# The second half of the queries in chunks of 256 instead of 512, in an attention + FFN kernel on one core

## The chip, the cores and the metric

The kernel runs on one core of one Trainium2 chip. The metric is the device time of one execution, in microseconds. Nearly all numbers below are medians of several executions, or come from one profiled execution (the span from its first to its last instruction is some 2 us shorter than its time).

The engines are called by their short names: PE is the matmul engine (TensorE), PEld its weight loads, DVE is VectorE, ACT is ScalarE, and SP issues most of the DMAs.

## The reference

S = 2048 tokens, D = 512, 32 heads of 16, an FFN of width F = 1792. All inputs are bfloat16.

```python
def _A_ref(x, wqkv, wo):                       # attention
    qkv = (x @ wqkv).reshape(B, S, 3, H, Dh).transpose(2, 0, 3, 1, 4)
    q, k, v = qkv[0], qkv[1], qkv[2]
    scores = einsum("bhqd,bhkd->bhqk", q, k) * (Dh ** -0.5)
    o = einsum("bhqk,bhkd->bhqd", softmax(scores), v)
    return o.transpose(0, 2, 1, 3).reshape(B, S, D) @ wo
def _B_ref(x, w_gate, w_up, w_down):           # gated FFN
    g = einsum("bsd,df->bsf", x, w_gate)
    u = einsum("bsd,df->bsf", x, w_up)
    return einsum("bsf,fd->bsd", sigmoid(g) * u, w_down)
x = A_x
h = x + _A_ref(_layernorm(x), A_wqkv, A_wo)
h2 = h + _B_ref(_layernorm(h), B_w_gate, B_w_up, B_w_down)       # the output
```

## The kernel before

The exponentials are the bulk of it: 32 heads x 2048 keys x 2048 queries. They are dealt out in **units** of 128 keys x 512 queries of one head, 2048 units in all. ACT does most of them with its Exp function, two or three units per instruction. DVE does 482 of them with integer arithmetic that leaves two operands to be summed up, so a DVE unit gives two value matmuls where an ACT unit gives one. PE makes the scores and the value sums and, in its gaps, everything else.

A head is only 16 wide, so one matmul would use a small part of the 128 x 128 array. Four heads are worked on side by side: head `j` of a group has rows 32j to 32j+31 of the array for its scores, and columns 32j to 32j+31 for its values. I call such a quarter a **strip**; `tile_position` names it.

```python
    QC = 512                # queries in a chunk
    NQC = S // QC           # four chunks
...
    def scores(n):          # the score matmuls of the n-th exponential instruction
        tiles.append(pick(want_dve(n)))
        ...
        for ui, (qc, g, kt, j) in enumerate(tiles[n]):     # chunk, group, key tile, strip
            mm = nc.tensor.matmul(pss[:, ui, :],
                                  lhsT=KT[g // 2][32 * j:32 * j + 32, kt * P:(kt + 1) * P],
                                  rhs=q[32 * j:32 * j + 32, :],
                                  start=True, stop=True, tile_position=(32 * j, 0))
...
    def in_rows(uns, limit):            # order of a batch of value matmuls: strip after strip
        out, rows, left = [], 0, list(uns)
        while left and len(out) < limit:
            used = set()
            for un in list(left):
                if un.u[3] not in used and len(out) < limit:
                    used.add(un.u[3]); left.remove(un); out.append(un)
            rows += 1
        return out, rows

    def av(limit, loose=60.0):          # a batch of value matmuls
        ...
        for un in uns:
            nc.tensor.matmul(acc[32 * j:32 * j + VW, :], lhsT=Vaug[:, kt, h, :], rhs=un.ap,
                             start=(c == 0), stop=(todo[qc, g, j] == 0), tile_position=(0, 32 * j))
...
    NPT, NPE = 36, 14                   # buffers for exponentials: 36 units, 14 more early on
```

The program's order is made ahead of time by a small scheduler in Python, which keeps an estimated clock for each engine and puts PE work between two score batches as long as it fits. Its main loop is this:

```python
        while T["P"] < lim - 100:
            ...
            r = ready_bg(0)             # first item of the background queue
            if early_on or (r is not None and tokens >= bg[0][2][1] and room("dense") >= bg[0][2][0]):
                used = try_bg(tokens, depth=3 if early_on else 1)
                ...
            uns, rows = in_rows(av_ready(60.0), 12)
            last = 0 < len(uns) == av_last()
            fit = int(room("av") // MM) * 4
            if (len(uns) >= 4 or last) and fit >= 4 and av(min(12, fit)):
                continue
            if quiet() and room("dense") >= MM and stir():      # a filler matmul
                continue
            T["P"] += 100
```

The background queue holds projections, and, once a chunk of queries has its attention, that chunk's output projection, layer norm and FFN. In the later part of the program the background has a single PSUM bank of 128 x 512 values. An FFN step fills it with a gate tile, ACT takes it out (tanh), then PE fills it with the up tile and DVE takes it out (product):

```python
    def ffn_up(qc, f):
        ...
        ps = pm_tile()                       # waits until the bank has been emptied
        gate_mm(ps, wgu[:, 0], ...)          # four 512-wide matmuls
        ja = pm_out(act(478, lambda: th.update({f: tanh_out(ps)}), st["mark"]))
        yield pe(2, pm_new)
        ps2 = pm_tile()                      # the same bank
        gate_mm(ps2, wgu[:, 1], ...)
        pm_out(dve(603, lambda: glu_out(hT, f, th[f], ps2), st["mark"], ja))
```

The FFN of the *last* chunk has no attention left to hide behind. After the last exponential comes a **tail**: last values, output projection, layer norm, gate/up, down, all for 512 queries.

## Time and profile before

| | before |
|---|---|
| time, median of 20 runs | 846.7 us (842.4 to 850.1) |
| span of the profiled run | 844.4 us |
| 1024 of 2048 exponential units started | 410.8 us |
| last unit started | 787.6 us |
| from there to the end (the tail) | 56.8 us |

The first fence is the page of the kernel before: the span, each engine's busy time and share of the span, and two of its groups of instructions (line, engine, operation, out<-in, shapes, count, then busy time, mean ns of one, and idle time just before them).

```profile
span 844.4 us, 14580 instructions
PE 757.3 (90%) x5697; PEld 232.8 (28%) x5792; DVE 779.5 (92%) x1446; ACT 765.8 (91%) x783; POOL 2.9 (0%) x7
...
L1189 ACT ACTIVATE pt<-PS 128x1024 f16<-128x1024 f32 (+2 forms) x663 | 699.8, 1190 | 28.4 <-PE PS L938 22.1
L1048 DVE TENSOR_SCALAR J<-PS 128x512 int16<-128x512 f32 x482 | 317.6, 683 | 14.8 <-PE PS L938 8.7
```

The three engines seem about equally busy. The view by windows separates the stages. Its columns are the window, its length, then busy time and instructions of each engine, the granted PE clock, the DMA share and GB/s. The windows are first half, second half and tail.

```profile
core 0: us, PE busy (x) PEld busy (x) DVE busy (x) ACT busy (x) POOL busy (x), PEclk, DMA share, GB/s
0.00:411.00 411.00, 356.81 (x2711) 107.55 (x2756) 385.07 (x730) 376.79 (x382) 2.90 (x7) 0.98 0.09 29
411.00:788.00 377.00, 353.33 (x2759) 104.17 (x2802) 371.90 (x674) 370.42 (x371) 0.00 (x0) 1.00 0.09 28
788.00:845.00 57.00, 47.12 (x233) 21.03 (x234) 22.53 (x44) 18.54 (x32) 0.00 (x0) 0.97 0.21 68
```

In the second half ACT and DVE are busy 98% and 99% of the time: the exponentials bound it. The tail is PE's: 47 of 57 us. PE's 353 of 377 us in the second half is not a measure of its need, because matmuls overlap, as the timeline of the kernel before shows (start, length, engine, line, operation, count):

```profile
330.81 0.39 PE L938 MATMUL PS<-QT_92,KT_86 32*128 32x512 bf16 x3
331.13 1.04 PE L710 MATMUL PS<-xnT_80,wgu 128*128 128x512 bf16 x4
332.10 0.39 PE L938 MATMUL PS<-QT_92,KT_86 32*128 32x512 bf16 x3
...
802.32 20.88 PE L710 MATMUL PS<-xnT_80,X 128*128 128x512 bf16 x94 [0.68 <-DVE xnT_80 L1328]
826.49 12.25 PE L1341 MATMUL PS<-wd,hT 128*128 128x512 bf16 x54
```

Three score matmuls on three strips together take 0.39 us, no longer than one takes: they start 3 to 4 ns apart. Four dense ones take 1.04 us, because dense matmuls start 216 ns apart. The Trainium skill ("Perfetto Trace Analysis", section Identifying the Most-Contended Engine) says that the busy share of the matmul row is not a good measure of how close PE is to its limit, because pipelined instructions look smaller in the trace. The last two lines are the gate/up and down matmuls of the tail, 20.9 and 12.3 us.

### The profile page before, as it was taken

To read this page: it belongs to the slowest core of one execution; us is meant where nothing else is said; L and a number is where in the kernel's file an instruction comes from. 1 tells how busy PE (TensorE), PEld (TensorE's weight loads), DVE (VectorE), ACT (ScalarE), POOL (GpSimd) and SP (SyncE) were. 2 spreads that over 40 slices of the span, in tenths; PEclk is the share of its full clock that TensorE was granted. 3 is DMA by queue.
4 is the path that set the end of the run, shared out by engine and by line. 5 is a ranking of instruction groups with operands and counts; after the bars stand their busy time and mean duration, and the time that the engine had idled before them with its cause. 6 is when DMAs were issued, how large, how long until landed. Compare 5 with 4: busy or idle time off the path is not lost.

```text
span 844.4 us, 14580 instructions
## 1 busy us (share of the span) xinstructions
PE 757.3 (90%) x5697; PEld 232.8 (28%) x5792; DVE 779.5 (92%) x1446; ACT 765.8 (91%) x783; POOL 2.9 (0%) x7
## 2 busy tenths in 40 slices
PE   4878988898899988999999999999898999998897
PEld 1322222222222222222222322222323222222343
DVE  7869899999999999999999999999999999999831
ACT  5839999899999999999999999999899999999631
POOL 1000000000000000000000000000000000000000
PEclk9978999999999999999999999999999999999999
DMA  6020000200000000020100011120100101000500
GB/s 211 1 88 1 1 1 1 63 2 1 2 1 1 14 1 26 26 63 27 51 13 26 2 39 37 51 63 15 38 14 1 51 26 50 1 8 13 175 7 28
DMA packets 38218, 26.16 MB, mean 31 GB/s; under 512 B 2560, under 2 KB 38144, under 8 KB 38144
## 3 DMA queue, kind: packets, MB, share of 16 engines
q1 hardware_dynamic: 36512, 23.99, 9.2%
q10 hardware_dynamic: 1632, 1.18, 0.4%
q8 instruction: 47, 0.77, 0.4%
q14 instruction: 27, 0.22, 0.1%
HBM read 23.07 MB, written 2.10 MB: 30 GB/s over the span
## 4 chain that ended last, share of the span: by engine, by line
DVE 34%; ACT 32%; PE 23%; issue 10%; DMA 0%; ACTq 0%; DVEq 0%
ACT pt L1189 28%; DVE J L1048 13%; DVE X L1082 6%; PE PS L710 6%; PE PS L938 6%; PE PS L1026 5%; DVE X L1072 3%; DVE X L1077 3%; ACT pe L1189 2%; PE PS L727 2%; DVE hT L722 2%; PE PS L1341 1%; DVE xs L982 1%; DVE Vaug L261 1%; PE PS L257 1%
## 5 line engine op out<-in xcount | busy, mean ns | idle before, releaser
L1189 ACT ACTIVATE pt<-PS 128x1024 f16<-128x1024 f32 (+2 forms) x663 | 699.8, 1190 | 28.4 <-PE PS L938 22.1
L1048 DVE TENSOR_SCALAR J<-PS 128x512 int16<-128x512 f32 x482 | 317.6, 683 | 14.8 <-PE PS L938 8.7
L1026 PE MATMUL PS<-pt,Vaug 128*17 128x512 f16 x1502 | 200.0, 383 | 3.1 <-DVE xs L982 2.3
L1082 DVE TENSOR_TENSOR X<-J,X 128x1024 f16<-128x1024 f16 (+1 forms) x246 | 159.2, 671 | 0.0
L1026 PE MATMUL PS<-X,Vaug 128*17 128x512 f16 x964 | 136.9, 383 | 6.1 <-DVE X L1082 2.6
L1026 PEld LDWEIGHTS <-Vaug 128*17 128x17 bf16 x2530 | 61.5, 89 | 127.7 <-issue 100.0
L710 PE MATMUL PS<-xnT_80,wgu 128*128 128x512 bf16 x304 | 88.3, 382 | 2.8 <-DVE hT L722 1.0
L1077 DVE TENSOR_SCALAR X<-J 128x2048 int16<-128x2048 int16 (+3 forms) x126 | 83.3, 661 | 0.1
L1072 DVE TENSOR_SCALAR X<-J 128x2048 int16<-128x2048 int16 (+3 forms) x126 | 83.0, 659 | 0.0
L722 DVE SCALAR_TENSOR_TENSOR hT<-th,PS 128x512 bf16<-128x512 f32 x56 | 38.1, 680 | 15.1 <-PE PS L710 15.1
L738 ACT ACTIVATE th<-PS 128x512 f32<-128x512 f32 x56 | 36.0, 643 | 14.7 <-PE PS L710 14.7
L727 PE MATMUL PS<-wd,hT 128*128 128x512 bf16 x157 | 45.2, 383 | 1.5 <-issue 1.3
L534 PE MATMUL PS<-wo_sb 128*128 128x512 bf16 x129 | 43.3, 393 | 1.7 <-issue 1.4
L938 PEld LDWEIGHTS <-KT_84 32*128 32x128 bf16 x512 | 21.0, 91 | 83.3 <-issue 77.7
L938 PE MATMUL PS<-QT_90,KT_85 32*128 32x512 bf16 x256 | 36.4, 387 | 6.7 <-ACT pt L1189 5.0
L938 PE MATMUL PS<-QT_92,KT_86 32*128 32x512 bf16 x256 | 36.1, 382 | 5.6 <-ACT pt L1189 4.5
L938 PE MATMUL PS<-QT_93,KT_86 32*128 32x512 bf16 x256 | 35.4, 383 | 5.6 <-ACT pt L1189 5.0
L938 PEld LDWEIGHTS <-KT_86 32*128 32x128 bf16 x512 | 19.5, 90 | 75.6 <-issue 75.1
L938 PEld LDWEIGHTS <-KT_85 32*128 32x128 bf16 x512 | 20.0, 91 | 73.5 <-issue 72.3
L938 PE MATMUL PS<-QT_95,KT_87 32*128 32x512 bf16 x256 | 35.7, 382 | 4.9 <-ACT pt L1189 3.8
L938 PE MATMUL PS<-QT_91,KT_85 32*128 32x512 bf16 x256 | 35.1, 382 | 5.1 <-ACT pt L1189 4.2
L938 PEld LDWEIGHTS <-KT_87 32*128 32x128 bf16 x512 | 19.8, 91 | 72.0 <-issue 71.2
(207 smaller groups left out, 575.5 us busy)
## 6 DMA issues: line engine op xcount, KB each, us to landing
wgu<-in_B_w_gate_dram SPq DMA_DIRECT2D x21, 256.0 KB, 2.8
wgu<-in_B_w_up_dram SPq DMA_DIRECT2D x21, 256.0 KB, 3.2
out_dram<-ob SPq DMA_DIRECT2D x16, 128.0 KB, 1.7
wd<-in_B_w_down_dram SPq DMA_DIRECT2D x1, 1792.0 KB, 7.3
xr<-in_A_x_dram SPq DMA_DIRECT2D x12, 128.0 KB, 3.1
X<-in_B_w_gate_dram SPq DMA_DIRECT2D x3, 512.0 KB, 3.8
X<-in_B_w_up_dram SPq DMA_DIRECT2D x3, 512.0 KB, 4.8
wv_sb<-in_A_wqkv_dram SPq DMA_DIRECT2D x1, 512.0 KB, 5.9
```

Source lines behind the costliest of these rows:

```text
L534: nc.tensor.matmul(PS[:, 1 + (st["ring"] + 1) % st["R"], :], lhsT=wo_sb[:, 0, 0:P], rhs=wo_sb[:, 0, :], start=True, stop=True)
L710: nc.tensor.matmul(ps, lhsT=w[:, d, :], rhs=hnT[:, d, :], start=(d == 0), stop=(d == DC - 1))
L722: nc.vector.scalar_tensor_tensor(out=hT[:, f, :], in0=th[:], scalar=1.0, in1=ps, op0=ALU.add, op1=ALU.mult)
L727: nc.tensor.matmul(ps, lhsT=hT[:, f, i * P:(i + 1) * P], rhs=wd[:, f, :], start=(f == 0), stop=(f == FC - 1))
L738: nc.scalar.activation(out=th[:], in_=ps, func=ACT.Tanh, scale=0.5)
L938: mm = nc.tensor.matmul(pss[:, ui, :], lhsT=KT[g // 2][32 * j:32 * j + 32, kt * P:(kt + 1) * P], rhs=q[32 * j:32 * j + 32, :], start=True, ...
L1026: nc.tensor.matmul(acc[32 * j:32 * j + VW, :], lhsT=Vaug[:, kt, h, :], rhs=un.ap, start=(c == 0), stop=(todo[qc, g, j] == 0), tile_positio ...
L1048: nc.vector.tensor_scalar(out=J[:, k, :], in0=src, scalar1=ZOFF, scalar2=0.0, op0=ALU.add, op1=ALU.max)
L1072: V.tensor_scalar(out=X[:, 0, 0:k, :], in0=J[:, 0:k, :], scalar1=POWER, scalar2=LITTLE, op0=ALU.bitwise_and, op1=ALU.bitwise_or)
L1077: V.tensor_scalar(out=X[:, 1, 0:k, :], in0=J[:, 0:k, :], scalar1=FRACTION, scalar2=HALF, op0=ALU.bitwise_and, op1=ALU.bitwise_or)
L1082: V.tensor_tensor(out=x, in0=J[:, a:b, :].bitcast(FP16), in1=x, op=ALU.mult)
L1189: ex = nc.scalar.activation(out=pt, in_=pss[:, 0:wa, :], func=ACT.Exp, scale=AS)
```

## The change

The intent is to halve the tail. If the last chunk has 256 queries, only their output projection, layer norm and FFN remain after the last exponential, and the other 256 can hide in the main loop. The last 1024 queries become four chunks of 256 (`SPAN` 2). To keep exponential instructions as long as they were, a unit then holds *two* key tiles x 256 queries. So what was one 512-wide matmul becomes two 256-wide ones, and they are issued as neighbours on the same strip. Along with it come changes in the scheduler's rules. Cut to its core:

```diff
+    SPAN = [1, 1] + [2] * (2 * (NQC - 2))      # chunks of 512, 512, 256, 256, 256, 256
+    CW = [QC // s for s in SPAN]               # their widths
...
 # scores: a unit is SPAN[qc] key tiles
-            mm = nc.tensor.matmul(pss[:, ui, :], lhsT=KT[...][..., kt * P:(kt + 1) * P],
-                                  rhs=q[32 * j:32 * j + 32, :], ..., tile_position=(32 * j, 0))
+            for i in range(SPAN[qc]):
+                k = kt * SPAN[qc] + i
+                nc.tensor.matmul(pss[:, ui, i * CW[qc]:(i + 1) * CW[qc]],
+                                 lhsT=KT[g // 2][32 * j:32 * j + 32, k * P:(k + 1) * P],
+                                 rhs=q[32 * j:32 * j + 32, cols(qc)],
+                                 start=True, stop=True, tile_position=(32 * j, 0))
...
 # values: the same, two neighbours on one strip
+            for i in range(SPAN[qc]):
+                nc.tensor.matmul(acc[32 * j:32 * j + VW, 0:w], lhsT=Vaug[:, kt * SPAN[qc] + i, h, :],
+                                 rhs=un.ap[:, i * w:(i + 1) * w], ..., tile_position=(0, 32 * j))
...
 # FFN: two feature tiles (each 128 x 256) share one bank, one tanh and one product
+            nc.vector.scalar_tensor_tensor(out=hT[:, f:f + k, cols(qc)],
+                in0=th[f][:].rearrange("p (k n) -> p k n", k=k), in1=ps2.rearrange(...), ...)
...
 # value batches only in full rows of four heads, but for the last of a group
-    def in_rows(uns, limit):
+    def in_rows(uns, limit, full=False):
+            if full and len(row) < live:
+                break
...
 # background: look one item deeper, let the item that holds the open bank go first,
 # put the job that empties the bank at the head of DVE's queue, projection + norm at the front
     def try_bg(tokens, loose=60.0, depth=1):
-        for i in range(depth):
+        owner = next((i for i, item in enumerate(bg) if item is st["open"]), None)
+        for i in range(depth) if owner is None else (owner,):
...
     def pm_out(job):
+        if job in dq:
+            dq.remove(job)
+            dq.insert(0, job)
...
-                queue(wo_ln(qc), ("wo", qc), 24)
+                queue(wo_ln(qc), ("wo", qc), 6 * k, 0)
...
 # main loop
-            r = ready_bg(0)
-            if early_on or (r is not None and tokens >= bg[0][2][1] and room("dense") >= bg[0][2][0]):
-                used = try_bg(tokens, depth=3 if early_on else 1)
+            if early_on or room("dense") >= (bg[0][2][0] if ready_bg(0) is not None else 2 * MM):
+                used = try_bg(tokens, depth=3 if early_on else 2)
...
-            if (len(uns) >= 4 or last) and fit >= 4 and av(min(12, fit)):
+            if fit >= 4 and av(min(12, fit), full=not last):
...
 # a second buffer for the rows h takes room from the exponentials' buffers
-    NPT, NPE = 36, 14
+    NPT, NPE = 30, 14
...
 # tail: 2 instead of 4 tiles of 128 queries
-    qc = NQC - 1
+    qc = NCH - 1
+    n = CW[qc] // P
```

Not shown in the cut are two more marks in the scheduler's list `STAGES`, by which it paces the background. From here on, "order rules" means the four scheduler changes: full rows, deeper look-ahead with the open bank's owner first, the promoted job, and the earlier projection and norm.

## The prediction

> **What bounds it now.** In the stage table (40 us stretches) from 200 to 760 us, ACT and DVE are each busy 39 to 40 of 40 us: the exponentials. PE shows 35 to 38.8 of 40, but its records overlap, so I added up what it really needs from start-to-start times in the trace: dense 128x512 matmuls start 216 ns apart; score or value matmuls on different 32-wide strips of the array start 3 to 4 ns apart (median 4 ns); two in succession on the same strip 215 ns apart (43 value pairs); a change between score, value and dense work costs about 95 ns. For the last 1024 queries (about 410 to 788 us) this gives 336 us of 378: PE has only some 11% to spare. After that comes a tail of 56 us (timeline: gate/up 20.9, down 12.3).
>
> **What the change moves.**
> - Tail: the last FFN serves 256 queries instead of 512. Gate/up 20.9 -> about 12 us, down 12.3 -> 6: about -18 us with the norm. The other half goes into the main loop.
> - ACT and DVE in the main loop: instruction counts of both programs show exponentials about equal (482 -> 470 units on DVE, ACT a little more), 7 more tanh/multiply pairs, 16 more group ends at half width, two more layer norms. Estimate +8 us on each.
> - PE: every 512-wide score or value matmul of the last two blocks becomes two of 256, and the program issues these two **one after the other on the same strip**, then goes to the next strip. PE starts in order: at 662.33 us a value matmul whose strip had been free for 0.19 us and that waited for no semaphore started only behind one held by its own busy strip. The Trainium skill ("TensorE: Matmul & The Clock Gate", Part 3) says the same: matmuls start and end in strict program order. So the second of a pair waits about 108 ns (half of 215) and holds back the next strip. Three score units: 108x4 = 432 instead of 222 ns. Four value units: 430 to 540 instead of 225 ns.
>
> Sum for the last 1024 queries, same rules applied to the new order: scores 76 -> 148 us, values 92 -> 157 (190 without the full-row rule), dense 105 -> 114, switches 63 -> 65: 336 -> 484 us.
>
> **Critical path.** 484 us is over ACT's and DVE's about 385, so PE becomes the bound in the second half, with some waits (94 to 97% useful): 500 to 515. First half hardly changed, 405 to 410. Total 407 + 504 + 38, plus 3 between span and time: 952 us.
>
> **What would show it.** Second half: ACT and DVE fall to about 75% busy, PE 95 to 100%; ACT's and DVE's idle time ends on score matmuls. Same-strip 256-wide neighbours start about 108 ns apart, and the next strip's 3 ns after the second. Last score matmul at about 915 us instead of 787; from there to the end about 38 instead of 56 us. First 400 us within 10 us of before.
>
> **What would make it wrong.** If the array let another strip start past a waiting matmul, PE would need about 345 us, and the result would be about 840: -18 tail, +8 main loop. If waits between PE and ACT add up in the static order (value batches of up to 40), 990.

## The result, and the profile after

| | before | after |
|---|---|---|
| time, median | 846.7 us (20 runs) | 837.0 us (10 runs, 835.1 to 840.8) |
| 1024 units started | 410.8 us | 408.7 us |
| last unit started | 787.6 us | 793.7 us |
| end of the last instruction | 844.4 us | 831.8 us |
| second half of the main loop | 376.8 us | 385.0 us |
| tail | 56.8 us | 38.1 us |

The ratio is 0.9895, with a 95% interval of 0.9875 to 0.9916. Here and below, a ratio is the mean time of one kernel's runs over that of the other's in the same rounds, so it isn't quite the ratio of the quoted medians. The result is a gain of 1%, where I had predicted a loss of 12%.

The page of the kernel after:

```profile
span 831.8 us, 19743 instructions
PE 727.4 (87%) x8183; PEld 288.4 (35%) x8275; DVE 779.2 (94%) x1525; ACT 766.0 (92%) x786; POOL 2.9 (0%) x7
...
L1233 ACT ACTIVATE pt<-PS 128x1024 f16<-128x1024 f32 (+2 forms) x661 | 706.3, 1253 | 29.6 <-PE PS L971 19.0
L1092 DVE TENSOR_SCALAR J<-PS 128x512 int16<-128x512 f32 x470 | 311.4, 681 | 11.9 <-PE PS L971 6.0
```

The windows of the kernel after, again first half, second half and tail:

```profile
0.00:409.00 409.00, 347.96 (x2743) 108.93 (x2792) 387.06 (x736) 375.64 (x383) 2.91 (x7) 0.99 0.10 31
409.00:794.00 385.00, 350.01 (x5220) 161.26 (x5268) 375.26 (x750) 377.18 (x377) 0.00 (x0) 1.00 0.16 46
794.00:832.00 38.00, 29.39 (x232) 18.21 (x225) 16.92 (x41) 13.19 (x28) 0.00 (x0) 0.92 0.31 100
```

PE has nearly twice the matmuls in the second half (5220 for 2759), and its row is no fuller than before (350 us). ACT and DVE are still 98% and 97% busy. So the main loop is bound by the exponentials as it was, and the tail is 19 us shorter. What went wrong with the prediction's sum is to be seen in the timeline of the kernel after:

```profile
599.38 0.84 PE L1069 MATMUL PS<-pt,Vaug 128*17 128x256 f16 x24
600.15 0.40 PE L971 MATMUL PS<-QT_88,KT_84 32*128 32x256 bf16 x6
600.48 0.41 PE L1069 MATMUL PS<-pt,Vaug 128*17 128x256 f16 x8
...
807.25 11.08 PE L724 MATMUL PS<-xnT_82,X 128*128 128x256 bf16 x96 [0.61 <-DVE xnT_82 L1358]
820.25 5.99 PE L1370 MATMUL PS<-wd,hT 128*128 128x512 bf16 x27
```

Six score matmuls, issued as pairs on three strips, are done in 0.40 us. One takes 0.27, so the last of the six started at most 0.13 us after the first. The starts in the trace are these, in ns after the first one, at 600.15 us:

```
record       1    2    3    4    5    6
start        0    6   13  120  125  132
```

The program's order is strip a, a, b, b, c, c. If matmuls started in that order, the second would have to wait some 109 ns for its own strip (half of the 216 of a 512-wide one), the third would start right behind it, and the last of the six would start after 334 ns. What the records show is three that start at once and three more a matmul later: each strip takes its own matmuls in order, and none waits for another strip.

The names in the records show the same without any timing. The built program issues one batch of eight value matmuls as four that read `X` (strips 0, 0, 64, 64) and then four that read `pt` (96, 96, 32, 32). In the trace of the kernel after, two of the `pt` ones start some 100 ns before the last two `X` ones:

```profile
761.26 0.28 PE L1069 MATMUL PS<-X,Vaug 128*17 128x256 f16 x2
761.27 0.28 PE L1069 MATMUL PS<-pt,Vaug 128*17 128x256 f16 x2
761.37 0.28 PE L1069 MATMUL PS<-X,Vaug 128*17 128x256 f16 x2
761.39 0.28 PE L1069 MATMUL PS<-pt,Vaug 128*17 128x256 f16 x2
```

Names out of the order of issue stand in 100 of the 353 value batches of this trace, and in 39 of the 330 of the kernel before: that trace held the answer before the prediction was made.

Over the whole trace, for every batch of one length, I compared the time from the first to the last start with both rules (the rules are computed with 109 ns between starts on a strip and 3 ns between strips):

| 256-wide batch, kernel after | measured median, ns | all in program order | order within a strip only |
|---|---|---|---|
| 6 score matmuls | 134 | 334 | 109 |
| 8 value matmuls | 134 | 446 | 109 |
| 16 value matmuls | 353 | 894 | 328 |
| 24 value matmuls | 571 | 1343 | 546 |
| 40 value matmuls | 1008 | 2240 | 982 |

With the right-hand rule PE's need for the last 1024 queries is 333 us before and 326 us after. With the middle rule it is 336 and 484, the two numbers of the prediction. (The Trainium skill, "TensorE: Matmul & The Clock Gate", Part 1, gives N / 2.4 GHz plus about 2.5 ns between starts, which is 215.8 ns for 512 and 109 for 256. The traces agree with both. For 512, (20.88 - 0.38) us over 95 steps in the tail before is 216 ns; these are 96 matmuls, of which two records are missing. For 256, dense ones in the second half after start mostly 109 ns apart, and in the batches of 24 the second matmul of a strip starts 114 ns after its first and each further one 109. In the tail after the mean is 114 ns, (11.08 - 0.27) us over 95 steps, because some of its steps take 131 to 152.)

### The profile page after: what moved, and what is told of

Same layout as the page of the kernel before. It is cut to its first block, busy times and chain, and to the rows that moved or that the text cites. A ratio compares the mean times of both kernels' runs of the same rounds, so it can differ in the third digit from the quotient of the medians.

```text
span 831.8 us, 19743 instructions
## 1 busy us (share of the span) xinstructions
PE 727.4 (87%) x8183; PEld 288.4 (35%) x8275; DVE 779.2 (94%) x1525; ACT 766.0 (92%) x786; POOL 2.9 (0%) x7
## 4 chain that ended last, share of the span: by engine, by line
ACT 39%; DVE 26%; PE 24%; issue 9%; DMA 1%; SPq 0%; ACTq 0%; DVEq 0%
ACT pt L1233 35%; DVE J L1092 10%; PE PS L971 7%; PE PS L743 5%; PE PS L724 4%; DVE X L1126 4%; PE PS L1069 3%; ACT pe L1233 2%; DVE hT L795 2%; DVE X L1116 2%; DVE X L1121 2%; ACT th L754 1%; PE PS L262 1%; DVE xs L1019 1%; DVE Vaug L266 1%
## 5 line engine op out<-in xcount | busy, mean ns | idle before, releaser
L1069 PE MATMUL PS<-pt,Vaug 128*17 128x256 f16 (+1 forms) x2300 | 175.6, 308 | 1.6 <-DVE xs L1019 1.4
L1069 PE MATMUL PS<-X,Vaug 128*17 128x256 f16 (+1 forms) x1410 | 138.6, 311 | 4.8 <-DVE X L1116 2.8
L1069 PEld LDWEIGHTS <-Vaug 128*17 128x17 bf16 x3777 | 83.8, 89 | 105.8 <-issue 96.9
L1121 DVE TENSOR_SCALAR X<-J 128x2048 int16<-128x2048 int16 (+2 forms) x127 | 81.7, 643 | 0.1
L1116 DVE TENSOR_SCALAR X<-J 128x2048 int16<-128x2048 int16 (+2 forms) x127 | 81.7, 643 | 0.0
L724 PE MATMUL PS<-xnT_80,wgu 128*128 128x256 bf16 (+1 forms) x325 | 60.5, 311 | 1.4 <-DVE hT L795 0.2
L724 PEld LDWEIGHTS <-wgu 128*128 128x128 bf16 x560 | 45.6, 98 | 44.3 <-issue 30.4
L743 PE MATMUL PS<-wd,hT 128*128 128x512 bf16 x182 | 52.9, 383 | 0.7 <-issue 0.5
L971 PEld LDWEIGHTS <-KT_84 32*128 32x128 bf16 x768 | 23.7, 91 | 78.7 <-issue 72.8
L971 PEld LDWEIGHTS <-KT_85 32*128 32x128 bf16 x768 | 25.1, 91 | 71.0 <-issue 68.8
L754 ACT ACTIVATE th<-PS 128x512 f32<-128x512 f32 (+1 forms) x63 | 41.1, 653 | 7.1 <-DVE hT L737 7.1
L971 PEld LDWEIGHTS <-KT_86 32*128 32x128 bf16 x768 | 24.4, 91 | 65.5 <-issue 64.2
L971 PE MATMUL PS<-QT_90,KT_85 32*128 32x256 bf16 (+1 forms) x384 | 36.0, 310 | 12.6 <-ACT pt L1233 11.3
L971 PEld LDWEIGHTS <-KT_87 32*128 32x128 bf16 x768 | 23.1, 91 | 63.6 <-issue 62.6
L971 PE MATMUL PS<-QT_91,KT_85 32*128 32x256 bf16 (+1 forms) x384 | 35.6, 310 | 10.7 <-ACT pt L1233 9.5
L971 PE MATMUL PS<-QT_95,KT_87 32*128 32x256 bf16 (+1 forms) x384 | 36.6, 308 | 7.1 <-ACT pt L1233 6.1
L971 PE MATMUL PS<-QT_92,KT_86 32*128 32x256 bf16 (+1 forms) x384 | 35.5, 308 | 7.3 <-ACT pt L1233 6.7
L971 PE MATMUL PS<-QT_94,KT_87 32*128 32x256 bf16 (+1 forms) x384 | 36.8, 308 | 5.6 <-ACT pt L1233 4.6
L971 PE MATMUL PS<-QT_93,KT_86 32*128 32x256 bf16 (+1 forms) x384 | 36.0, 308 | 6.3 <-ACT pt L1233 5.1
```

Of the source, the lines that this page charges most:

```text
L724: nc.tensor.matmul(ps[:, 0:CW[qc]], lhsT=w[:, d, :], rhs=HN[qc][:, d, cols(qc)], start=(d == 0), stop=(d == DC - 1))
L743: nc.tensor.matmul(ps, lhsT=hT[:, f, q:q + P], rhs=wd[:, f, :], start=(f == 0), stop=(f == FC - 1))
L754: nc.scalar.activation(out=th[:, 0:ps.shape[-1]], in_=ps, func=ACT.Tanh, scale=0.5)
L971: nc.tensor.matmul(pss[:, ui, i * CW[qc]:(i + 1) * CW[qc]], lhsT=KT[g // 2][32 * j:32 * j + 32, k * P:(k + 1) * P], rhs=q[32 * j:32 * j + ...
L1069: nc.tensor.matmul(acc[32 * j:32 * j + VW, 0:w], lhsT=Vaug[:, kt * SPAN[qc] + i, h, :], rhs=un.ap[:, i * w:(i + 1) * w], start=(c + i == 0 ...
L1116: V.tensor_scalar(out=X[:, 0, 0:k, :], in0=J[:, 0:k, :], scalar1=POWER, scalar2=LITTLE, op0=ALU.bitwise_and, op1=ALU.bitwise_or)
```

## The experiments

Twelve kernels were run. Each diff is against the kernel after, but for one that is said to be against the kernel before. "1664 units" and "last unit" are times in the profiled run at which that many exponential units had been started.

### 1. e1: the two halves of a pair not as neighbours

```diff
-            for i in range(SPAN[qc]):
-                nc.tensor.matmul(..., tile_position=(32 * j, 0))
+        for ui, i in sorted(((ui, i) for ...), key=lambda e: (e[1], e[0])):   # all first halves, then all second
+                nc.tensor.matmul(..., tile_position=(32 * j, 0))
 # the same in each row of the value matmuls
```

> The changed kernel, but the two 256-wide matmuls of a unit are no longer neighbours: score tiles and rows of value units go first half of every strip, then second half of every strip. Theory A (each 32-wide strip of the array takes its matmuls in its own order; a busy strip does not hold up the others): no change, ratio to before 0.985 to 0.993, and score tiles of six matmuls still span about 135 ns from first to last start. Theory B (strict program order over all strips, the rule of the prediction): the second of a pair holds up the next strip in the changed kernel and not here, so this should be clearly faster than the changed kernel, by 5% or more.

Measured: 836.6 us, ratio 0.987 (0.985 to 0.990), like the kernel after. Its value batches of 8, 16 and 24 span 125, 343 and 561 ns, each some 10 ns less than in the kernel after. In-order starts would have made this kernel far faster than the kernel after; putting the pairs apart changes nothing that can be seen in the time. So the order of the strips within such a short stretch is free.

### 2. e2: value batches sorted by strip

```diff
-        for un in uns:
+        for un in sorted(uns, key=lambda un: un.u[3]):
```

A batch of 24 now has six matmuls on one strip, then six on the next, and so on.

> The changed kernel, but every batch of value matmuls is issued strip by strip (all of strip 0, then all of strip 1 and so on), so up to six neighbours (256 wide) or three (512 wide) lie on one strip. Theory A without a limit on how far ahead the array looks: no change, 0.985 to 0.993 of before. Theory A with a short look-ahead (a few matmuls): batches of 24 take longer than their 546 to 570 ns, the kernel is slower than the changed one by 2 to 10%. Theory B: value batches run almost one strip after another, about 150 us more PE time in all, about 960 us or more.

Measured: 854.1 us, ratio 1.008 (1.006 to 1.011): some 17 us slower than the kernel after. The last unit started at 816.8 us and the tail was unchanged (36.7 us). Batches of 16 (runs of four on one strip) span 372 ns, as good as the 353 of mixed order. Batches of 24 (runs of six) span 1237 ns instead of 571. The starts of such a batch begin with 0, 115, 224, 230, 334, 344, 443: the second strip begins two matmuls late. The window of the second half:

```profile
412.00:817.00 405.00, 374.55 (x5211) 181.75 (x5252) 379.57 (x750) 381.08 (x378) 0.00 (x0) 1.00 0.15 43
```

ACT's share falls to 94% over these 405 us. Some 36 batches of 24, each 0.67 us longer, make 24 us at most, and the second half of the main loop took 19 us more than after (404.4 to 385.0). So order across strips is free only over a short look-ahead.

### 3. e8: runs of five on one strip

```diff
+        # five neighbours on one strip, then the next strip; what is left over after them
+            place[k] = (seen[p] // 5, p, k)
+        for i, k, kw in sorted(emit, key=lambda e: place[e[1]]):
```

> The changed kernel, value batches issued in runs of five neighbours on one strip, then five on the next strip, then what is left. Rule to be tested, from the second experiment, where runs of four cost nothing (batch of 16: 372 ns) and runs of six made a batch of 24 take 1238 instead of 571 ns: on each strip one matmul runs and three wait, a fourth waiting one blocks all that follow. Then a batch of 24 takes about 8 x 109 = 872 ns plus some start gaps, 870 to 910. If four may wait, 571 to 600; if two, about 1200. One time near 845 us.

Measured in one look: 844.1 us (a single run, so its state isn't known). Batches of 24 span 909 ns, batches of 16 again 372. With e2 this fixes the depth for these value matmuls. If one matmul of a strip runs and three more can wait without holding back other strips, then a run of five delays the next strip by one matmul, a run of six by two. For the last start of a batch of 24 that makes, with 109 ns each, 3 x 1 + 5 = 8 steps = 872 ns for fives, and 3 x 2 + 5 = 11 steps = 1199 ns for sixes. Measured: 909 and 1237. Runs of four cost nothing (372 ns). The kernel after puts only two on a strip before it goes on to the next, so it lies well within this. Whether it is the matmuls themselves that are counted, or the weight load that goes with each, these runs do not show.

### 4. e3 and e6: the order rules alone, with chunks of 512

```diff
-    SPAN = [1, 1] + [2] * (2 * (NQC - 2))
+    SPAN = [1] * NQC
 # and the tail of the kernel before, for 512 queries
```

> The changed kernel's order rules (full value rows of four heads, layer norm first in the background, background look-ahead of two, the second normalised-input buffer) with four chunks of 512 and the old end for 512 queries. If the gain comes from the shorter end (56.8 to 38.1 us in the two traces), paid back in part by the main loop of the last two blocks (+8 us), then this keeps only the 2 us that the first half won, perhaps a little more in the second: 842 to 846 us, ratio 0.994 to 0.999, with an end of about 56 us. Rival: the order rules bring the gain, then this is at 0.99 or below with the end still at 56 us.

Measured: 848.3 us, ratio 1.001, and a **wrong result** (relative error 0.24). The load of the last residual rows went into a buffer that the last query projections still needed: it was issued at 588 us and the projections lasted to 626 us. The time missed the expectation, too (842 to 846 us). The mended kernel puts them elsewhere:

```diff
-    xl = xnT[3]
+    xl = xnT[2]
```

> The third experiment again with its fault mended (the residual rows of the last chunk are loaded into a buffer that is no longer read, the result must be right). Times as there: ratio 0.999 to 1.003, end about 57 us, main loop 788 to 791 us. So the order rules alone gain nothing. Rival: they gain 3 us or more.

Measured: correct, 846.6 us, ratio 1.001 (0.999 to 1.003). The last unit starts at 786.9 us, and the tail is 57.2 us, as before. The order rules with the 30 buffers make no difference to the kernel before.

### 5. e10: the kernel before with 30 buffers

```diff
 # against the kernel before
-    NPT, NPE = 36, 14
+    NPT, NPE = 30, 14
```

> The kernel before, with 30 instead of 36 buffers for exponentials (the changed kernel gave six up for a second buffer of residuals). If the fewer buffers are what made the fifth experiment slow, this is slower than before by 0.3% or more. If not: ratio 0.998 to 1.002.

Measured: 855.5 us, ratio 1.0084 (1.0056 to 1.0112); last unit at 797.7 us. So six fewer buffers cost the old kernel 0.8%, and e6 is "no change" only because the order rules pay that back.

### 6. e5: the chunks of 256 alone, with the old order rules

```diff
-        if job in dq: dq.remove(job); dq.insert(0, job)
-        owner = next((i for i, item in enumerate(bg) if item is st["open"]), None)
-                queue(wo_ln(qc), ("wo", qc), 6 * k, 0)
+                queue(wo_ln(qc), ("wo", qc), 6 * k)
-                used = try_bg(tokens, depth=3 if early_on else 2)
+                used = try_bg(tokens, depth=3 if early_on else 1)
-            if fit >= 4 and av(min(12, fit), full=not last):
+            if (len(uns) >= 4 or last) and fit >= 4 and av(min(12, fit)):
```

> The changed kernel's four chunks of 256 and its shorter end, but with the order rules of before: any four value units are issued at once instead of full rows of four heads, background work is taken only from the head of its list, the layer norm waits its turn. Theory C (the gain is the shorter end alone; the rules only move work): end 38 us, main loop as long as in the changed kernel or up to 3 us longer, 836 to 841 us, ratio 0.988 to 0.993. Rival D (the chunks need the full rows, because value matmuls in broken rows cost PE time when PE has little to spare): main loop 8 us or more longer, ratio 0.997 or above.

Measured: 851.1 us, ratio 1.0053 (1.003 to 1.0076). The last unit starts at 804.6 us, 11 us later than in the kernel after, and the tail is 44 us. A part is one stall, shown by a window and by the waits from 446 to 456 us of this kernel (engine, line, what it waited for, total us, times, longest):

```profile
448.00:454.00 6.00, 1.67 (x22) 0.71 (x25) 4.79 (x19) 0.38 (x1) 0.00 (x0) 0.79 0.01 1
...
ACT pt L1229 <- PE PS L1065: 6.4, 1, 6.4
...
PE PS L1065 <- DVE X L1122: 3.4, 1, 3.4
```

ACT waits 6.4 us for an exponential buffer to be freed by value matmuls (line 1065), and these wait for a DVE product, which stands behind the small steps of a layer norm in DVE's queue. Nothing like it is in the second half of the kernel after, whose longest wait of ACT for value matmuls is 2.3 us. Of the 11 us, 4.2 arise before the 1024th unit (412.9 us; 408.7 in the kernel after), where the chunks are 512 wide in both, and 6.7 in the second half, where the stall is. The 6 us of the tail I did not take apart. Theory C (836 to 841 us) missed; the size was that of rival D, but e9 below speaks against the full rows as its reason.

With e6 and e10 this gives a table of two by two, all four with 30 buffers (ratio to the kernel before with its 36):

| | old order rules | new order rules |
|---|---|---|
| chunks of 512 | 1.0084 (e10) | 1.0009 (e6) |
| last 1024 queries in chunks of 256 | 1.0053 (e5) | 0.9895 (the kernel after) |

One way to add it up: +0.84% for the buffers, -0.75% for the order rules, -1.14% for the chunks. The chunks by themselves gain 0.31% with the old rules, so most of their gain depends on the new ones. Two reservations: the 0.31% are not clear of noise (the intervals of e5 and e10 overlap, and they ran in different rounds), and e10 is the kernel before, so it differs from e6 in the pacing marks and the second buffer for `h` as well as in the order rules.

### 7. e4: only the last 512 queries in chunks of 256

```diff
-    SPAN = [1, 1] + [2] * (2 * (NQC - 2))
+    SPAN = [1] * (NQC - 1) + [2, 2]
```

> Only the last 512 queries are split in two chunks of 256; the block before goes as one chunk of 512. The end stays at 38 us. Splitting one block less saves 8 pairs of group ends (0.58 us of DVE each pair by the trace: 2 x 1.15 instead of 1.72 us, estimate 4.6 us), one set of small layer-norm steps and weight loads: if these are what the main loop pays, this is 2 to 4 us faster than the changed kernel, ratio to before 0.984 to 0.988. Rival: small chunks help the main loop by themselves (work of the FFN spread evenly), then it is slower than the changed kernel, 0.991 or more.

Measured: correct, 845.3 us, ratio 0.999 (0.997 to 1.001). The expectation missed; the rival was right. At 1664 units this kernel was ahead (646.6 us; after 650.5), and at the last unit it was behind (799.8; after 793.7). The windows from there to the last unit, first of this kernel, then of the kernel after:

```profile
646.00:800.00 154.00, 141.80 (x2013) 63.41 (x2037) 145.11 (x283) 144.45 (x150) 0.00 (x0) 0.97 0.17 50
```

```profile
650.00:794.00 144.00, 133.16 (x2057) 65.76 (x2071) 140.39 (x270) 141.19 (x144) 0.00 (x0) 1.00 0.20 57
```

For the same number of units it has 10 us more, in which DVE is busy 5 us more and ACT 3 us more, and both have idle time (94%). In these last 512 queries it has to hide the FFN of 768 queries (a whole chunk of 512 and then one of 256), where the kernel after hides that of 512. That this is the cause is my reading; no run changes the FFN's load alone. The clock also dipped in this profile (0.97).

### 8. e7: one feature tile of 256 in a bank

```diff
     def ffn_up(qc, f):
-        k, w = SPAN[qc], CW[qc]
+        k, w, m = 1, CW[qc], 2 // SPAN[qc]
 # one tile per bank, one tanh and one product for each; estimates halved
```

> The changed kernel, but in the chunks of 256 the FFN takes one feature tile (256 wide) per PSUM bank instead of two. In the main loop 21 tanh and 21 products of 512 become 42 and 42 of 256: by the trace 0.37 instead of 0.60 us and 0.42 instead of 0.68 us each, so about 3 us more of ACT and 3.4 us more of DVE. If ACT and DVE are the bound: 2 to 4 us slower than the changed kernel, ratio 0.992 to 0.995. If the single bank that the background has left makes twice as many turns a wait for PE: 6 us or more slower.

Measured: 865.0 us, ratio 1.021 (1.019 to 1.024), the slowest of all: without this part the change loses 2%. The rival was right, and its size was well above its lower bound of 6 us. At the last unit (804.7 us) a part of the background FFN was left over and ran alone. The window and the timeline there:

```profile
805.00:868.00 63.00, 46.03 (x303) 27.25 (x293) 19.79 (x48) 16.30 (x36) 0.00 (x0) 0.78 0.27 85
...
814.51 1.01 PE L724 MATMUL PS<-xnT,wgu 128*128 128x256 bf16 x4 [0.58 <-DVE hT L737]
...
815.57 0.38 ACT L754 ACTIVATE th<-PS 128x256 f32<-128x256 f32 x1 [2.69 <-PE PS L724]
816.00 1.01 PE L724 MATMUL PS<-xnT,wgu 128*128 128x256 bf16 x4 [0.47 <-ACT th L754]
...
817.12 0.42 DVE L737 SCALAR_TENSOR_TENSOR hT<-th,PS 128x256 bf16<-128x256 f32 x1 [2.66 <-PE PS L724]
```

The one bank is filled (1.01 us), emptied by ACT (0.38), filled (1.01), emptied by DVE (0.42), with nothing beside it: 3.1 us for 128 features of 256 queries. PE's granted clock is low there (0.78 over the window, 0.50 from 812 to 819 us; that the gaps are the reason is my reading), and four 256-wide matmuls take 1.01 us, where four of them at full clock (at 601.63 us of the kernel after) take 0.61. The bank is turned over as often for 256 queries as for 512 if it holds one tile; with two tiles in it the number of turns per query stays what it was.

### 9. e9: batches of any rows

```diff
+            uns, rows = in_rows(av_ready(60.0), 12)
-            if fit >= 4 and av(min(12, fit), full=not last):
+            if (len(uns) >= 4 or last) and fit >= 4 and av(min(12, fit)):
```

> The changed kernel with one of its order rules undone: value matmuls are issued again as soon as four units are ready, in whatever rows they make. The fifth experiment (all order rules undone) lost 1.6% on the changed kernel, in part by one stall of 7 us near 450 us where background order matters. If the full rows are what PE needs in the chunked blocks: value time rises there, ratio to before 0.997 or more. If it is the background order (layer norm first, look-ahead of two) that matters: this keeps the gain, 0.988 to 0.992.

Measured: 837.6 us, ratio 0.989 (0.987 to 0.992), and a **wrong result** (relative error 0.24). The cause is in the program's order, not on the chip: its built program, run in the simulator, gives the same error, and one of the 16 key tiles of `Vaug` is wrong, tile 10, which holds the values of tile 11. Early in the program the PSUM bank of tile 10 is filled again before it has been copied out. By its time, the rule of full rows isn't what makes the order rules pay. I give this with the reservation that no run has this one fault mended.

### 10. e11 and e12: the tail's projections earlier, and the last units on ACT

In the tail of the kernel after, the last value matmuls wait for DVE's part of the last exponentials, and the six output projections that need nothing from them come afterwards. The first kernel moves these six ahead:

```diff
+    for p in range(NP - 1):
+        for i in range(n):
+            nc.tensor.matmul(hps[i], lhsT=OT[qc, p][...], rhs=wo_sb[:, p, :], start=False, stop=False)
     while avq:
         flush()
         av(8, 1e12)
```

> The changed kernel with six of the last eight output-projection matmuls issued before the last value matmuls, where PE waits for DVE (794.5 to 799.4 us); in the changed kernel they come after, 0.43 us apart at half clock. Expected: end 38.1 to about 35.5 us, ratio to before 0.985 to 0.988. If PE was not what that stretch waits for: no change.

Measured: 838.1 us, ratio 0.988 (0.985 to 0.991), tail 38.0 us: no change, and the expectation missed. My edit was in the wrong place. The waits for DVE lie before it, in the main loop, which has by then emitted all value matmuls, so the six still ran after them, and at half clock (0.50 granted from 804 to 805 us). The timeline of e11:

```profile
802.72 0.39 PE L1069 MATMUL PS<-X,Vaug 128*17 128x256 f16 x2 [0.21 <-DVE X L1126]
...
803.68 1.04 PE L1314 MATMUL PS<-xnT,ident 128*128 128x512 bf16 x2
804.51 2.15 PE L1317 MATMUL PS<-wo_sb,ot 128*128 128x512 bf16 x6
```

The second kernel keeps this edit and also lets DVE start no new group of units once no more than twelve units remain to be issued (466 units on DVE instead of 470):

```diff
-                 and pend <= 2600)
+                 and pend <= 2600 and (bool(half) or sum(b.left() for b in blocks) > 12))
```

> As the eleventh, and the last four exponential units go to ACT instead of DVE (DVE ends its last exponentials 4.6 us after ACT in the changed kernel). ACT gains 1.7 us of work, DVE loses about 4.6. Expected: 2 us better than the eleventh, ratio to before 0.982 to 0.986.

Measured: correct, 833.8 us, ratio 0.984 (0.982 to 0.987). The last unit starts at the same time as in e11 (797.8 and 797.9 us), and the tail is 32.5 us instead of 38.0. Its timeline and window:

```profile
799.69 1.46 PE L1317 MATMUL PS<-wo_sb,ot 128*128 128x512 bf16 x6
...
798.00:831.00 33.00, 26.29 (x184) 16.68 (x183) 12.48 (x33) 13.35 (x28) 0.00 (x0) 0.96 0.21 66
```

No wait for DVE stands before the projections any more, and they run at nearly full clock (1.46 us for the six; 2.15 in e11). Since e11 in the same rounds shows that the move by itself does nothing, the gain comes with giving ACT the last units; whether that alone, without the move, gains as much was not run. This version is faster than both kernels: 13.7 us below the runs of the kernel before in its rounds. It wasn't run in the same rounds as the kernel after. Against that one's 0.9895 its ratio to the kernel before is about half a per cent lower, and the two intervals just miss each other.

## Why the prediction was wrong

**The step that failed** is the one that the prediction put as "PE starts in order", from which it took that "the second of a pair waits about 108 ns (half of 215) and holds back the next strip". What the runs show in its place: a matmul that waits for its own strip does not hold back other strips, unless more than three of them wait on one strip. The kernel after and e1 show the first part (six paired score matmuls start within some 135 ns, and putting the pairs apart gains nothing), e2 and e8 the second, for value matmuls. From the failed step came PE's need of 484 us, which is 326 us with the right rule, and from that the predicted second half of 504 us, which took 385.

**How I came to believe it.** I took two supports for two, and they were one. The first was the Trainium skill ("TensorE: Matmul & The Clock Gate", Part 3, What overlaps and what doesn't): "MATMULs are pc-monotone in start AND end — strict FIFO, no reordering". The second was a place in the trace of the kernel before. Seven 512-wide value matmuls, issued on strips 64, 96, 0, 32, 0, 32, 64 in this order, start there like this, in ns after 661.926 us:

```
record        1    2    3    4    5    6    7
start         0    3  183  186  220  398  407
```

I laid the seven starts beside the seven instructions in program order, and read that the last one, on strip 64, which had been free since about 216, started only at 407, behind the two before it. But putting them side by side in program order already assumes what was to be shown. It also can't be right: it gives strip 0 its two matmuls at 183 and 220, 37 ns apart, where two of this width on one strip need some 215. The reading that fits has the record at 220 as the *second matmul of strip 64* (220 after its first), which went past the two that waited; 398 is 183 + 215 and 407 is 186 + 221. So the evidence that I quoted for the rule speaks against it. A page that the prediction did not look at pointed the other way, too: the Trainium skill's "TensorEngine Tiling (Array Packing)", Key Properties, says that tiles operate independently and that different tiles can execute matmuls in parallel. The runs agree, up to the depth of three waiting.

**What was right.**
- The tail: predicted from 56 to 38 us, measured from 56.8 to 38.1. Gate/up went from 20.9 to 11.1 us (predicted 12), down from 12.3 to 6.0 (predicted 6).
- The bound before: ACT and DVE in the main loop, PE in the tail.
- The first half: predicted 405 to 410 us, measured 408.7.
- The sentence on what would make it wrong ("If the array let another strip start past a waiting matmul ... about 840: -18 tail, +8 main loop"). The array does, the tail gave -18.7 us, the second half took +8.2 us, and the time is 837.0.

**What was right in sum only.** The +8 us was put on both ACT and DVE as work. The windows show that the work grew by 6.8 us on ACT (370.4 to 377.2) and 3.4 on DVE (371.9 to 375.3); the rest of the 8 us is idle time.

**What was not foreseen.** I gave no cost to the six fewer buffers, which cost the old kernel 0.8% (e10). I gave no gain to the order rules, which pay that back with chunks of 512 and without which the chunks of 256 gain only 0.3%, within the noise (e5, e10). And I did not say that two feature tiles in a bank would decide the sign of the whole: without it the change would have been 2% slower (e7).

**What stays open.** Which of the order rules matters most (e9 speaks against the full rows, but its result was wrong); how e4's loss divides between the FFN's load and the rest; and why the tail of e5 is 6 us longer.

## What to carry to other kernels

Before a rule about an engine's order carries a prediction, look for a record that the rule forbids. Do not pair records with instructions by program order when that order is in question; pair them by what can't be otherwise, here the 215 ns that one strip needs between two starts. When work is cut into smaller pieces to shorten the tail, see to it that the turns of a scarce resource do not multiply with the pieces: here the one PSUM bank had to be filled with two tiles, or the gain of 1% would have been a loss of 2%. And the tail that remains deserves a look at which engine gets the last pieces: leaving the last four units to ACT, with six output projections moved ahead, took another 4 us off (e11 to e12: 838.1 to 833.8).

## What the Trainium skill lacked or had wrong

- "TensorE: Matmul & The Clock Gate", Part 3, What overlaps and what doesn't, has matmuls as strictly first in, first out in start and end. For matmuls on different strips the runs show otherwise: paired score matmuls (a, a, b, b, c, c) start within some 135 ns, where that order would need 334; in 100 of 353 value batches of the kernel after the records' names are out of the order of issue; and putting the pairs apart made no difference clear of noise (836.6 and 837.0 us). "PSUM — Partial Sum Buffer", Engine vs sequencer instructions, says the same of program order, and the same runs differ from it.
- No page that I read gives the depth to which strips are independent. For 256-wide value matmuls the runs fit one running and three waiting per strip: runs of four on a strip cost nothing (16 matmuls in 372 ns), runs of five and six do (24 in 909 and in 1237 ns, instead of 571).
- "TensorEngine Tiling (Array Packing)", Key Properties, is right that tiles run independently, but doesn't say that this ends where more than three matmuls wait on one tile (the same numbers).
